# A linear-attention and feed-forward kernel: w3 laid out for 32x32 block turns on VectorE, seven products for one more chunk, another opening and another order of work

## The chip, the core and the metric

The kernel runs on one core of one Trainium2 chip. The metric is the device time of one execution in microseconds (us), lower is better. The engines are named as in the profile: PE (TensorE, matrix products; PEld are its weight loads), DVE (VectorE), ACT (ScalarE), POOL (GpSimd) and SP (SyncE, which here only issues DMAs). Each engine works through its own list of instructions in order and waits on semaphores for the others.

## The reference

Two blocks follow each other. The first is a recurrent linear attention over 4 batches, 8 heads, 768 steps and a head size of 48:

```python
for t in range(S):
    cur = np.einsum('bhd,bhe->bhde', u[None] * kt, vt)
    y[:, :, t] = np.einsum('bhd,bhde->bhe', rt, state + cur)
    state = w[None, :, :, None] * state + np.einsum('bhd,bhe->bhde', kt, vt)
```

Its output, reordered to x of 3072 tokens by 384, goes through a multiplicative feed-forward block. `w1` and `w2` are 384 x 1024, `w3` is 1024 x 1024, `w_out` is 1024 x 384:

```python
a = x @ w1
b = x @ w2
h = a * b @ w3
return (h @ w_out)
```

The weights arrive as 64-bit floats, so their transfers carry twice the bytes of 32-bit ones.

## The kernel before, in words

**Units and chunks.** The sequence is cut into 6 chunks of 128 steps. A chunk of one batch is a unit, so there are 24 units; the four units of a chunk give the 512 tokens of one feed-forward step. For each unit `scale` multiplies k and r by powers of w (tile `pn_in`, which the opening computes), `adds` and `products` form the sums over time, `state` carries the state on, `with_state` and `with_pairs` give y, and `turn_y`/`put_y` turn it into `xT`. From unit 5 on, k and r are turned by blocks on VectorE (`turn_blocks`, L492), written to memory (`turn_out`, L496) and read back in another order (`turn_places`, L504).

**Weights.** Nothing in the kernel multiplies with 64-bit floats. 32 pieces are loaded by `fetch` (L229) into three raw buffers in turn, `raws[i % 3]`: pieces 0 to 7 are strips of w1 and w2 (768 KB each), 8 to 15 are 128-row blocks of w_out (384 KB), 16 to 31 are half blocks of 128 rows of w3 (512 KB). Five steps rebuild 32-bit floats from the two words of each number: `magnitude` and `low` on ScalarE, `sign`, `high` and `total` on VectorE. A buffer is free for piece i + 3 when `low` has read it.

**Folding.** Since nothing stands between w3 and w_out, their product w34 is computed once: for each block j of 128 rows, `fold_turn` turns w3's block with eight 128x128 transposes on TensorE (L398), `fold_put` copies them out of PSUM (L403), `fold` multiplies by w_out (L408, eight products of 384 columns), `fold_take` copies the result to w34. The tiles `w3n` and `w3T` share four buffers of 4 KB per partition.

**Products.** For chunks 0 and 1 the products of x with w1 and w2 are plain ones (`product_ab`, L740: three products of 512 columns for each of 8 blocks of features and each weight). For chunks 2 to 5 seven half-size products take the place of eight (`product_half`, L885 and L889, 256 columns each, with `gather_half`), over two of the three blocks of 128 inputs; they need sums of quarters of the weights (`sums_of_w`) and of x (`sums_of_x`). The product of h with w34 is always done in seven parts (`product`, L798, `gather`).

**Order.** A string of 1406 words, `ORDER`, is the whole program of PE, ACT, DVE and SP for this case. A word is a step and its indices: `W.9` issues piece 9, `M`, `N`, `H`, `L`, `Q` convert it, `G.j.h`, `K.j.h`, `F.j`, `X.j` fold block j, `a.c.j.part`/`b.c.j.part` are plain products, `pa`/`pb` and `ga`/`gb` half-size ones, `P`, `E`, `D` the products with w34, their sums and stores, `k`, `T`, `R`, `U`, `A`, `S`, `V`, `Y`, `yt`, `x`, `y`, `z` and others the steps of a unit, `Z.n.i` n products that only keep TensorE busy. Steps on different engines wait for each other through the tiles they share; each engine keeps the order of the string. The order was written by a planner outside the kernel.

**Opening.** Before the string, VectorE builds powers of w by doubling in the tile `both`; two copies double its width (L297, L298), TensorE turns eight 128x128 blocks (L303), and ScalarE copies the two halves g into `pn_in` (L304). A branch then picks this program or a general one for other values of w; only the first is run here.

Of the kernel before, what the change touches and what calls it, by code (L numbers as in the profile page):

```python
# [8 lines left out]
F32 = mybir.dt.float32  # L9
# [14 lines left out]
k.0 uw Z.1.0 R.0 vs.0 T.0 k.1 kr.2 U.0 t.0 v.2 r.0 i.0 T.1 j.0 ku.0 A.0 R.1 N.0 v.1 Au.0 t.1 r.1 S.0 m.0 kr.3 ku.1  # L24
mo.0 k.2 Z.4.0 A.1 M.0 Au.1 fe.0 R.2 W.1 m.1 vs.2 T.2 mo.1 U.2 W.2 t.2 H.0 V.0 r.2 Y.0 v.3 A.2 i.2 j.2 ku.2 U.1 yt.0
kr.4 i.1 j.1 S.2 L.0 Au.2 k.3 yx.0 vs.1 Z.1.0 R.3 m.2 T.3 M.1 mo.2 S.1 fe.2 fe.1 t.3 V.2 N.1 V.1 r.3 H.1 Y.2 A.3 W.3
Q.0 ku.3 yt.2 N.2 kr.5 vs.3 Z.2.0 Au.3 Y.1 m.3 yx.2 Z.2.0 U.3 mo.3 M.2 yt.1 v.5 i.3 k.4 S.3 yx.1 L.1 a.0.0.0 fe.3 H.2
Q.1 M.3 V.3 W.4 T.4 N.3 Y.3 R.4 H.3 kr.6 t.4 yt.3 b.0.1.0 r.4 j.3 ku.4 k.5 A.4 v.6 cz.1 L.3 Au.4 x.5 b.0.0.0 yx.3 L.2
Q.3 a.0.1.1 M.4 N.4 W.5 Q.2 vs.5 W.6 H.4 c.0.0.0 c.0.1.1 Z.3.0 b.0.2.2 m.4 v.4 L.4 mo.4 W.7 vs.6 Q.4 d.5 a.0.2.2
u.0.0.0 y.5 N.5 M.5 H.5 U.5 c.0.2.2 a.0.1.0 u.0.2.2 L.5 ub N.6 M.6 Q.5 b.0.1.1 vs.4 W.8 H.6 b.0.4.2 c.0.1.0 u.0.1.0  # L30
L.6 u.0.1.1 Q.6 W.9 M.7 N.7 a.0.4.2 H.7 z.5 e.5 L.7 f.5 Q.7 M.8 a.0.7.2 c.0.4.2 N.8 H.8 M.9 N.9 W.10 L.8 H.9 W.11 Q.8
L.9 b.0.6.2 Q.9 c.0.7.2 W.12 h.5 kr.7 l.5 d.6 e.6 f.6 a.0.0.1 M.10 N.10 H.10 b.0.7.2 N.11 M.11 kr.8 u.0.4.2 L.10 H.11
c.0.0.1 L.11 Q.10 N.12 M.12 Q.11 a.0.5.2 W.13 H.12 L.12 W.14 k.7 Q.12 W.15 b.0.0.1 d.7 c.0.5.2 e.7 kr.10 f.7 A.5
u.0.0.1 b.0.3.2 i.5 M.13 N.13 H.13 N.14 L.13 m.5 M.14 W.16 H.14 a.0.6.2 M.15 Q.13 L.14 N.15 W.17 H.15 Q.14 L.15 Q.15
W.18 c.0.6.2 j.5 b.0.5.2 u.0.6.2 M.16 N.16 H.16 u.0.7.2 M.17 a.0.3.2 N.17 L.16 H.17 W.19 Q.16 L.17 N.18 M.18 W.20 Q.17
G.0.0 c.0.3.2 H.18 G.0.1 K.0.0 U.4 u.0.3.2 L.18 k.6 K.0.1 W.21 F.0 N.19 M.19 kr.9 Q.18 H.19 N.20 M.20 i.4 L.19 H.20
W.22 Q.19 L.20 Q.20 M.21 W.23 N.21 G.1.0 X.0 H.21 G.1.1 K.1.0 U.6 j.4 K.1.1 G.2.0 x.6 L.21 F.1 K.2.0 W.24 Q.21 M.22
y.6 N.22 H.22 k.8 L.22 M.23 W.25 N.23 H.23 Q.22 L.23 N.24 W.26 G.2.1 Q.23 M.24 S.4 z.6 x.7 K.2.1 G.3.0 X.1 G.3.1 fe.4
H.24 K.3.0 F.2 M.25 N.25 u.0.5.2 L.24 H.25 K.3.1 Q.24 L.25 y.7 Q.25 M.26 W.28 N.26 H.26 W.27 d.8 l.6 e.8 kr.11 G.4.1
G.4.0 L.26 x.8 A.6 K.4.0 V.4 i.6 X.2 F.3 Y.4 cz.0 v.7 M.28 m.6 K.4.1 j.6 z.7 M.27 N.28 H.28 Q.26 L.28 Q.28 N.27 H.27  # L40
S.5 X.3 G.6.0 vs.7 fe.5 y.8 G.5.0 K.6.0 W.29 P.0.0.0 L.27 Q.27 W.30 V.5 W.31 l.7 yt.4 Y.5 G.5.1 g.6 yt.5 v.8 F.4 z.8
N.29 M.29 f.8 yx.4 H.29 yx.5 N.30 L.29 d.9 K.5.0 Q.29 K.5.1 N.31 g.7 S.6 e.9 G.6.1 fe.6 V.6 K.6.1 U.7 Y.6 v.9 M.30 A.7
k.9 F.6 M.31 X.4 m.7 kr.12 l.8 i.7 j.7 vs.8 x.9 vs.9 H.30 y.9 H.31 L.30 Q.30 L.31 U.8 X.6 Q.31 S.7 A.8 fe.7 k.10 V.7
yt.6 z.9 m.8 G.7.0 yx.6 i.8 G.7.1 K.7.0 F.5 j.8 K.7.1 g.8 x.10 v.10 s.0.1.0 y.10 s.0.1.1 Y.7 s.0.1.2 l.9 f.9 d.10 yt.7
X.5 e.10 kr.13 ps f.10 yx.7 g.9 s.0.1.3 z.10 d.11 b.1.0.2 e.11 vs.10 f.11 d.12 e.12 a.1.0.2 b.1.1.2 c.1.0.2 u.1.0.2
a.1.5.2 a.1.1.2 c.1.5.2 b.1.2.2 c.1.1.2 u.1.1.2 a.1.2.2 a.1.4.2 c.1.2.2 u.1.2.2 S.8 c.1.4.2 U.9 fe.8 l.10 A.9 k.11
b.1.4.2 i.9 kr.14 j.9 m.9 x.11 U.10 A.10 u.1.4.2 y.11 V.8 k.12 F.7 v.11 i.10 kr.15 j.10 m.10 Y.8 z.11 x.12 vs.11
a.1.3.2 B.0 X.7 E.0.0.0 s.0.0.0 y.12 B.1 a.1.6.2 s.0.0.1 c.1.3.2 B.3 B.2 s.0.0.2 P.0.0.2 c.1.6.2 wb.0 wb.1 P.0.1.4
s.0.0.3 wa.0 P.0.0.3 wa.1 wb.3 P.0.1.2 wa.3 E.0.0.2 U.11 E.0.0.3 P.0.0.4 k.13 x.13 P.0.1.0 E.0.0.4 y.13 b.1.6.2
E.0.1.0 E.0.1.2 b.1.5.2 u.1.6.2 P.0.1.1 u.1.5.2 s.1.0.0 P.0.0.5 s.1.0.1 s.1.0.3 a.1.7.2 s.1.0.2 E.0.1.1 E.0.0.6  # L50
E.0.0.5 D.0.0.0 P.0.0.1 wa.2 c.1.7.2 P.0.0.6 E.0.0.1 b.1.3.2 E.0.0.7 D.0.0.1 P.0.1.6 u.1.3.2 P.0.1.3 P.1.0.0 E.0.1.3
E.0.1.4 yt.8 E.1.0.0 P.0.1.5 g.10 b.1.7.2 E.0.1.6 E.0.1.7 f.12 yx.8 D.0.1.1 d.13 e.13 kr.16 P.1.1.0 u.1.7.2 s.1.1.0
P.1.0.4 s.1.1.1 E.1.1.0 s.1.1.3 P.1.0.2 s.1.1.2 wb.2 P.1.0.6 E.1.0.2 E.0.1.5 D.0.1.0 P.1.0.3 P.1.0.5 E.1.0.3 E.1.0.4
P.1.1.1 E.1.0.6 E.1.0.5 D.1.0.0 P.1.1.4 E.1.1.1 P.1.0.1 P.1.1.2 E.1.0.1 E.1.0.7 D.1.0.1 S.9 E.1.1.2 P.1.1.3 fe.9 l.11
z.12 V.9 E.1.1.3 Y.9 A.11 P.1.1.5 i.11 j.11 yt.9 m.11 v.12 P.1.1.6 yx.9 E.1.1.6 g.11 E.1.1.4 E.1.1.5 S.11 D.1.1.0
E.1.1.7 S.10 D.1.1.1 fe.11 V.11 fe.10 l.12 f.13 V.10 v.14 Y.11 U.12 v.13 vs.12 Y.10 yt.11 k.14 z.13 pa.2.0.0 yx.11
x.14 A.12 ga.2.0.0 yt.10 i.12 pa.2.0.1 yx.10 m.12 g.12 j.12 xs.2.0 S.12 y.14 xs.2.1 U.13 fe.12 xs.2.2 ga.2.0.5 V.12
xs.2.3 g.13 pa.2.0.5 d.14 v.15 e.14 kr.17 pa.2.1.4 Y.12 f.14 pa.2.0.4 ga.2.0.1 d.15 l.13 e.15 pa.2.0.6 ga.2.0.3 vs.13
A.13 z.14 f.15 yt.12 ga.2.0.2 i.13 pb.2.0.0 vs.15 m.13 yx.12 pa.2.0.7 j.13 g.14 k.15 pa.2.0.3 ga.2.0.4 kr.18 x.15
vs.14 S.13 U.14 ga.2.0.7 fe.13 y.15 d.16 V.13 gb.2.0.0 k.16 pa.2.0.2 l.14 v.16 Y.13 e.16 kr.19 f.16 pb.2.0.5 ga.2.0.6  # L60
d.17 pa.2.1.0 e.17 gb.2.0.1 pb.2.0.6 x.16 z.15 pb.2.0.1 gb.2.0.2 vs.16 pb.2.0.3 gb.2.0.5 y.16 A.14 gb.2.0.7 yt.13 m.14
ga.2.1.0 pb.2.0.4 g.15 i.14 pa.2.1.5 j.14 pa.2.1.1 gb.2.0.3 ga.2.1.1 f.17 yx.13 d.18 l.15 pb.2.0.7 e.18 pb.2.1.0
ga.2.1.5 gb.2.0.4 z.16 pa.2.1.6 gb.2.0.8 U.15 ga.2.1.2 pb.2.0.2 k.17 x.17 kr.20 pa.2.1.3 gb.2.0.6 y.17 ga.2.1.3
s.2.0.0 pa.2.1.7 s.2.0.2 pa.2.1.2 ga.2.1.4 ga.2.1.7 gb.2.1.0 s.2.0.1 s.2.0.3 pb.2.1.4 ga.2.1.6 S.14 pb.2.1.1 fe.14
l.16 z.17 V.14 gb.2.1.5 A.15 Y.14 P.2.1.0 m.15 i.15 v.17 yt.14 E.2.1.0 j.15 pb.2.1.5 yx.14 g.16 S.15 U.16 fe.15 V.15
k.18 A.16 v.18 gb.2.1.1 P.2.0.0 Y.15 kr.21 l.17 gb.2.1.3 m.16 vs.17 pb.2.1.7 x.18 E.2.0.0 yt.15 pa.3.0.0 yx.15 i.16
y.18 g.17 pb.2.1.6 j.16 f.18 S.16 xs.3.0 U.17 xs.3.1 gb.2.1.2 A.17 fe.16 xs.3.2 vs.18 V.16 i.17 pb.2.1.3 v.19 j.17
z.18 m.17 gb.2.1.4 pb.2.1.2 gb.2.1.7 gb.2.1.8 ga.3.0.0 gb.2.1.6 pa.3.0.4 vs.19 s.2.1.0 pa.3.0.5 s.2.1.2 pa.3.0.1
ga.3.0.1 s.2.1.1 ga.3.0.3 l.18 s.2.1.3 pa.3.0.6 xs.3.3 ga.3.0.5 pa.3.0.2 k.19 ga.3.0.2 x.19 pb.3.0.0 Y.16 ga.3.0.6
y.19 d.19 S.17 e.19 kr.22 U.18 fe.17 f.19 A.18 i.18 V.17 pa.3.0.7 v.20 m.18 pa.3.0.3 ga.3.0.4 z.19 j.18 Y.17 P.2.1.1  # L70
ga.3.0.7 k.20 gb.3.0.0 d.20 P.2.0.3 e.20 vs.20 x.20 kr.23 P.2.0.2 E.2.1.1 P.2.0.5 y.20 E.2.0.2 E.2.0.3 l.19 pb.3.0.5
# [34 lines left out]
def kernel(  # L106
# [60 lines left out]

# [885 lines left out]
```

## Time and profile before

| | us |
|---|---|
| median of 3 runs | 507.02 |
| lowest and highest run | 500.76, 507.63 |
| profiled execution, time | 501.81 |
| profiled execution, span | 500.1 |
| PE busy | 483.8 |
| DVE busy | 319.5 |
| ACT busy | 202.7 |
| first product of chunk 1 starts at | 139.65 |
| last PE instruction ends near | 494.8 |

The profile shows one execution. A matrix product of 32-bit floats appears as two records, and records of neighbours overlap, so costs of products are read from the start-to-start distance of a row of them, not from the mean duration. Busy shares are means over stages that have different limits; a stretch of the span tells more. In a table of stretches "x" counts instructions, PEclk is the clock that was granted to TensorE, and DMA share is the mean over the 16 DMA engines. Packets that cross a border of a short stretch can lift the share above 1.

### The profile page before, as it was taken

What the parts mean: (1) busy time and instruction counts of PE and PEld (TensorE: products, weight loads), DVE (VectorE), ACT (ScalarE), POOL (GpSimd) and SP (SyncE); (2) the same over time, 40 slices, a digit from 0 to 9 for tenths busy, and PEclk for the clock granted to TensorE, in tenths of its full rate; (3) what the DMA queues carried; (4) which work ended last, traced back from release to release, by engine and by line L of the source; (5) the groups of instructions that cost most, each with busy time, mean ns of one, the idle gap of its engine ahead of it and who ended that gap; (6) DMA issues with size and microseconds to landing.
All of it is one profiled execution on the core that took longest, in us unless ns stands there. A gap on an engine that the chain in (4) does not pass through costs nothing.

```text
span 500.1 us, 11978 instructions
## 1 busy us (share of the span) xinstructions
PE 483.8 (97%) x5066; PEld 384.4 (77%) x5066; DVE 319.5 (64%) x648; ACT 202.7 (41%) x470; POOL 4.4 (1%) x17
## 2 busy tenths in 40 slices
PE   6899999989999999999999999999999999999995
PEld 5786545657644586898888889989998889888895
DVE  5799999985951874539967894539462564524352
ACT  3887646768632100206852633062422232322300
POOL 3000000000000000000000000000000000000000
PEclk9999999999999999999999999999999999999999
DMA  8969787896620600216734435002300020000002
GB/s 193 241 167 287 209 224 227 250 262 172 159 64 1 174 33 20 59 49 177 167 108 108 113 99 139 32 33 70 90 33 31 1 81 17 27 25 0 2 1 69
DMA packets 97279, 52.72 MB, mean 105 GB/s; under 512 B 78144, under 2 KB 88640, under 8 KB 97216
## 3 DMA queue, kind: packets, MB, share of 16 engines
q1 hardware_dynamic: 96592, 51.85, 37.6%
q8 instruction: 42, 0.69, 0.6%
q14 instruction: 21, 0.17, 0.1%
q10 hardware_dynamic: 624, 0.00, 0.1%
HBM read 39.65 MB, written 12.19 MB: 104 GB/s over the span
## 4 chain that ended last, share of the span: by engine, by line
PE 86%; DMA 5%; DVE 4%; ACT 2%; issue 1%; SPq 0%; ACTq 0%; DVEq 0%
PE ps_accB L885 8%; PE ps_b L740 7%; PE ps_a L740 7%; PE ps_w L408 5%; PE ps_a11b L798 3%; PE ps_s1t L798 3%; PE ps_s4b L798 3%; PE ps_s3t L798 3%; PE ps_a22t L798 3%; PE ps_s2t L798 3%; PE ps_a12b L798 3%; PE ps_Ab L885 3%; PE ps_accB L889 3%; PE ps_a L551 3%; PE ps_accC L885 3%; PE ps_Aa L885 3%
## 5 line engine op out<-in xcount | busy, mean ns | idle before, releaser
L740 PE MATMUL ps_b<-xT,w 128*128 128x512 f32 (+1 forms) x108 | 44.4, 550 | 0.9 <-ACT a L746 0.7
L740 PE MATMUL ps_a<-xT,w 128*128 128x512 f32 (+1 forms) x108 | 43.7, 547 | 0.0
L408 PE MATMUL ps_w<-wo,w3T 128*128 128x384 f32 x128 | 43.0, 489 | 0.0
L885 PE MATMUL ps_accB<-x,w 128*128 128x256 f32 x128 | 36.5, 387 | 0.0
L740 PEld LDWEIGHTS ps_a<-xT,w 128*128 128x128 f32 x108 | 20.3, 190 | 20.5 <-issue 18.4
L408 PEld LDWEIGHTS ps_w<-wo,w3T 128*128 128x128 f32 x128 | 23.7, 190 | 15.1
L452 ACT ACTIVATE ynat<-vnat,dg 128x48 f32<-128x48 f32 x144 | 34.4, 325 | 0.8 <-PE ps_x L710 0.7
L740 PEld LDWEIGHTS ps_b<-xT,w 128*128 128x128 f32 x108 | 19.9, 190 | 18.7 <-issue 15.8
L508 ACT COPY kT<-tt 128x1024 f32<-128x1024 f32 x19 | 19.9, 1047 | 23.3 <-PE ps_y L671 21.0
L382 ACT ACTIVATE t<-raw 128x512 uint32<-128x512 uint32 (+2 forms) x32 | 22.6, 710 | 14.6 <-DVE wo L378 6.7
L885 PEld LDWEIGHTS ps_accB<-x,w 128*128 128x128 f32 x128 | 23.2, 190 | 5.0 <-ACT u2a L902 1.1
L422 DVE TENSOR_TENSOR krs<-krin,pn_in 128x768 f32<-128x768 f32 x24 | 22.9, 953 | 5.9 <-PE ps_a L544 3.3
L749 DVE TENSOR_TENSOR abt<-ps_b,a 128x512 f32<-128x512 f32 (+1 forms) x18 | 11.2, 628 | 20.5 <-ACT a L746 14.0
L746 ACT COPY a<-ps_a 128x512 f32<-128x512 f32 (+1 forms) x18 | 9.5, 535 | 33.4 <-PE ps_a L740 33.3
L716 ACT COPY xT<-ps_x 128x384 f32<-128x384 f32 x24 | 11.4, 478 | 28.8 <-PE ps_x L710 28.6
L678 ACT COPY vodd<-vnat 64x192 f32<-64x192 f32 x48 | 16.8, 350 | 13.8 <-DMA vnat<-in_v_dram 12.8
L551 PE MATMUL ps_a<-kT 64*64 64x64 f32 x768 | 16.8, 222 | 3.0 <-ACT kT L508 1.7
L813 ACT COPY m<-ps_a11b 128x192 f32<-128x192 f32 x12 | 3.8, 320 | 38.7 <-PE ps_a11b L798 38.7
L492 DVE STREAM_TRANSPOSE tr<-krs 128x768 f32<-128x768 f32 x19 | 18.4, 970 | 1.1 <-DMA scratch<-tr 0.9
L602 DVE COPY_PREDICATED AT<-later,ps_a 128x512 f32<-128x512 int32 x24 | 17.5, 730 | 2.5 <-PE ps_a L572 1.4
L889 PE MATMUL ps_accB<-xT,w 128*128 128x256 f32 x64 | 19.0, 379 | 0.0
L889 PE MATMUL ps_accC<-xT,w 128*128 128x256 f32 x64 | 19.0, 379 | 0.0
(191 smaller groups left out, 1069.0 us busy)
## 6 DMA issues: line engine op xcount, KB each, us to landing
raw<-in_moe_w_dram SPq DMA_DIRECT2D x16, 512.0 KB, 4.9
scratch<-tr SPq DMA_DIRECT2D x19, 384.0 KB, 3.1
raw<-in_moe_w_dram SPq DMA_DIRECT2D x8, 768.0 KB, 5.8
tt<-scratch SPq DMA_DIRECT2D x38, 128.0 KB, 3.1
krin<-in_k_dram SPq DMA_DIRECT2D x24, 192.0 KB, 3.8
krin<-in_r_dram SPq DMA_DIRECT2D x24, 192.0 KB, 4.3
vnat<-in_v_dram SPq DMA_DIRECT2D x24, 192.0 KB, 3.8
raw<-in_moe_w_out_dram SPq DMA_DIRECT2D x8, 384.0 KB, 3.6
```

Source lines behind the costliest of these rows:

```text
L382: nc.scalar.activation(out=part["t", i], in_=words(i)[0], func=COPY, scale=2.0 ** -29)
L408: nc.tensor.matmul(ps, lhsT=w3T[j][:, kc, :], rhs=wo[kc], start=(kc == 0), stop=(kc == KF - 1))
L422: nc.vector.tensor_mul(krs[n % NS][:, which, :, :D], kr[:, which], pn[:, which, :, :D])
L452: nc.scalar.activation(out=ynat[n][:, h, :], in_=vnat[n % NV][:, h, :], func=COPY, scale=dg[n][:, h:h + 1])
L492: nc.vector.transpose(out=blocks[n].rearrange("x m e t -> x e m t"), in_=krs[n % NS][:, :, :, :D])
L508: nc.scalar.copy(out=turned(n).rearrange("x g p (z t) -> x (g p) z t", t=Q), in_=tts.rearrange("x z e t -> x e z t"))
L551: nc.tensor.matmul(upper(n)[rows(a ^ i), i, p, :], lhsT=kT[n][rows(i), p, rows(a)], rhs=rT[n][rows(i), p, rows(a)], start=True, stop=True)
L602: nc.vector.copy_predicated(AT[n], later.bitcast(I32)[:, None, None, :].to_broadcast([C, 2, NP, T]), upper(n))
L740: nc.tensor.matmul(ps, lhsT=(w1 if x == "a" else w2)[:, z, q, js], rhs=xT[c][:, q, ts], start=(q == 0), stop=(q == KM - 1))
L798: nc.tensor.matmul(ps, lhsT=operand(c, j // 2, a)[:, j % 2, m * C:(m + 1) * C], rhs=w34[:, KH * (x == 1) + j, :DH] if x < 2 else made[b][: ...
L885: nc.tensor.matmul(ps, lhsT=quarter(w, g, i, x), rhs=(b11, b21, b22, t4, b12, t2, t3)[x], start=x in (0, 4) and i == 0, stop=True, skip_gr ...
L889: nc.tensor.matmul(ps, lhsT=wide_of[w][:, g + half * HZ, 2, i * P:(i + 1) * P], rhs=xT[c][:, 2, side * TH:(side + 1) * TH], start=False, s ...
```

## The change

Three parts and a new order.

**w3 and w_out are loaded in another layout.** A piece of w3 is now two transfers. Each brings 32 rows of w3, and each of the four groups of 32 partitions takes another quarter of the columns. In that layout a turn of 32x32 blocks within each group gives what a 128x128 transpose gave, with the inner index of the product permuted; the rows of w_out are loaded with the same permutation. `fold_turn` becomes one block turn on VectorE for each half, and `fold_put` (word `K`) goes.

```diff
+            if i < NAB + KF:
+                queue.dma_start(out=landed[i] if i < NAB else landed[i][:, 0], in_=pieces[i])
+            else:
+                j, z = divmod(i - NAB - KF, NW3)
+                for f in range(2):
+                    queue.dma_start(out=landed[i][:, 0, f * DF // NBLOCK:(f + 1) * DF // NBLOCK],
+                                    in_=moe_w3[j * P:(j + 1) * P].rearrange("(f r) (q x) -> f q r x", r=Q, q=NBLOCK)[2 * z + f])
...
-    pieces = [src for src, _ in strips] + [moe_w_out[j * P:(j + 1) * P, None, :] for j in range(KF)] \
+    pieces = [src for src, _ in strips] + [moe_w_out.rearrange("(q c x) n -> c q x n", q=P // Q, x=Q)[j] for j in range(KF)] \
...
-            pst["w3", j, h] = ps = psT.tile([P, KF // 2, P], F32, tag="t", name=f"ps_w3T{j}_{h}")
-            for q in range(KF // 2):
-                kc = h * (KF // 2) + q
-                nc.tensor.transpose(ps[:, q, :], w3n[j][:, kc * P:(kc + 1) * P], ident)
+            if j not in w3T:
+                w3T[j] = wide_pool.tile([P, KF, P], F32, tag="w3", bufs=4 if fast else 3, name=f"w3T{j}")
+            by = w3n[j].rearrange("x (f c r) -> x f c r", f=NBLOCK, r=Q)[:, 2 * h:2 * h + 2]
+            nc.vector.transpose(out=w3T[j].rearrange("x c (f r) -> x f c r", r=Q)[:, 2 * h:2 * h + 2], in_=by)
```

Here `P` is 128, `Q` is 32, `NBLOCK` is 4, `KF` is 8 and `NW3` is 2.

**Chunk 1's products with w1 and w2 are half-size ones too** (`pa.1`, `pb.1`, `ga.1`, `gb.1` in place of `a.1`, `b.1`, `c.1`, `u.1`). The sums of w1, w2 and x that they need take the four shared buffers of w3 when the folding is done (`kept`, `more_kept`), since the memory of the other pools is full then.

```diff
-                made["w", w] = [room().tile([P, HZ, STRIP], F32, name=f"w{w}{i}") for i in (1, 2, 4)]
+                made["w", w] = [kept(3 * (w == "b") + i) for i in range(3)]
...
-                made["x", c] = [room().tile([P, TH], F32, tag=f"x{i}", name=f"x{i}_{c}") for i in (2, 3, 4)]
+                made["x", c] = [more_kept(i * TH, TH) for i in range(3)]
```

**The opening is rewritten at its end.** `both` isn't doubled any more; 16 products with the identity write each of the 8 blocks to both halves of the partitions, and the second copy into `pn_in` is VectorE's. A constant tile shares its memory with a raw buffer. The first unit's `scale` is split into k and r.

```diff
-        nc.vector.tensor_copy(out=both[:, 0, :, T:], in_=both[:, 0, :, :T])
-        nc.scalar.copy(out=both[:, 1, :, T:], in_=both[:, 1, :, :T])
-
...
-                nc.tensor.transpose(ps[:, p, :], both[:, g, p, :], ident)
-            nc.scalar.copy(out=pn_in[:, g].rearrange("t h d -> t (h d)"), in_=ps.rearrange("x p t -> x (p t)"))
+                for a in range(2):
+                    nc.tensor.matmul(ps[rows(a), p, :], lhsT=both[:, g, p, :T], rhs=ident, start=True, stop=True)
+            put = nc.vector.tensor_copy if g else nc.scalar.copy
+            put(out=pn_in[:, g].rearrange("t h d -> t (h d)"), in_=ps.rearrange("x p t -> x (p t)"))
```

**The order** is a new string of 1426 words. Ahead of chunk 1's products it now has all of the folding, with `F.7` before `F.5`, and the first of the products with w34. Fillers fall from 13 products to 3. Part of it, where the folding ends:

```
... Q.30 G.7.0 s.0.1.0 L.31 Q.31 l.7 s.0.1.1 vs.7 z.8 G.7.1 S.6 X.6 wa.0 U.7 g.7 A.7 fe.6 wa.2 V.6 i.7 F.7 ...
... V.7 F.5 v.10 m.8 f.8 z.9 x.10 g.8 d.9 wb.3 Y.7 vs.10 y.10 i.8 kr.12 j.8 yt.7 B.0 X.5 P.0.1.0 yx.7 l.9
xs.1.0 xs.1.1 P.0.1.1 xs.1.2 E.0.1.0 z.10 xs.1.3 E.0.0.0 s.0.0.0 pb.1.0.4 ...
```

## The prediction, made before the result was known

> **What bounds the kernel now.** I read the page's busy shares first, then a table of stretches of the span, the chain that ended last, the waits, and last the DMA issues.
>
> ```profile
> span 500.1 us, 11978 instructions
> PE 483.8 (97%) x5066; PEld 384.4 (77%) x5066; DVE 319.5 (64%) x648; ACT 202.7 (41%) x470; POOL 4.4 (1%) x17
> DVE  5799999985951874539967894539462564524352
> DMA  8969787896620600216734435002300020000002
> ```
>
> TensorE is the bound by its share, but the third and fourth line say that VectorE and the DMA engines are nearly as full over the first quarter. The stretches show it in microseconds (stretch, length, busy time of PE, PEld, DVE, ACT, POOL, clock, DMA share, GB/s):
>
> ```profile
> 10.50:75.00 64.50, 61.83 (x888) 41.68 (x888) 56.29 (x101) 45.47 (x96) 0.00 (x0) 1.00 0.81 225
> 75.00:111.50 36.50, 33.94 (x275) 21.21 (x276) 32.99 (x62) 24.02 (x43) 0.00 (x0) 1.00 0.83 245
> 111.50:139.65 28.15, 27.96 (x416) 19.31 (x414) 21.50 (x45) 21.25 (x55) 0.00 (x0) 1.00 0.57 159
> 139.65:172.00 32.35, 32.25 (x263) 16.44 (x264) 14.81 (x29) 7.16 (x19) 0.00 (x0) 1.00 0.33 73
> 44.00:46.00 2.00, 2.00 (x6) 0.90 (x5) 2.00 (x5) 1.42 (x3) 0.00 (x0) 1.00 1.03 367
> 76.00:78.00 2.00, 2.00 (x6) 0.88 (x5) 1.90 (x5) 0.00 (x0) 0.00 (x0) 1.00 0.87 283
> 118.00:120.00 2.00, 2.00 (x8) 1.21 (x7) 1.91 (x4) 1.98 (x6) 0.00 (x0) 1.00 1.10 350
> ```
>
> 139.65 us is where TensorE begins the products of chunk 1; I call that moment X. Before X, VectorE is busy 110.8 of 129.15 us, from 75 to 111.5 us even 33.0 of 36.5. The DMA engines are 81 to 83% busy until 111.5 us. After X only TensorE is full. Over 69 to 106 us the chain runs through weight pieces, not through TensorE:
>
> ```profile
> 73.37 5.06 DMA raw<-in_moe_w_dram
> 80.61 4.98 DMA raw<-in_moe_w_dram
> 91.53 5.11 DMA scratch<-tr
> 97.97 6.35 DMA tt<-scratch
> ```
>
> SyncE's queue waits, before it may issue a piece, for the step `low` that empties the raw buffer (first line); the others are the pieces and their time to land:
>
> ```profile
> SPq L234 <- ACT t L382: 46.1, 23, 5.7
> raw<-in_moe_w_dram SPq DMA_DIRECT2D x16, 512.0 KB, 4.9
> raw<-in_moe_w_out_dram SPq DMA_DIRECT2D x8, 384.0 KB, 3.6
> ```
>
> So the pieces are now paced by the conversion that frees buffers. How fast are the 16 engines? The last three stretches above are mostly weights: 367/1.03, 283/0.87 and 350/1.10 GB/s are 318 to 356 at full share, 20 to 22 GB/s per engine. In the trace's packet records the median 2 KB packet takes 84 ns (24.4 GB/s), a 3 KB packet 121 ns, a 192 B packet 15 ns.
>
> [...] This trace has the operation itself in f32: 128x768 in 970 ns (L492), which I use. [...] Here the granted clock is 1.00 in every stretch of work[...].
>
> **The change, part by part.**
>
> *TensorE.* The 64 transposes of w3 (L398) go: eight cost 0.87 us back to back, four 0.44, so 7.0 us. Fillers (L921) fall from 13 products to 3: a pair of records is 0.216 us, so 2.2 us of filler. Chunk 1 as seven products: per weight and half of the features, 12 products of 512 columns at 0.859 us (2.58 us for three) become 22 of 256 columns at 0.431 (1.29 for three): 10.31 against 9.48, four times, 3.3 us less. Sum 12.5 us, if TensorE stays the bound.
>
> *VectorE and ScalarE.* 16 puts of w3T leave ScalarE (16 x 0.58 = 9.3 us). 16 block turns of 128x512 come onto VectorE: from 970 ns for 768 elements, 0.65 us each, 10.4 us (0.60 to 0.75 as ends). Seven weight sums (0.69 each), `B.0` and two halves of x now stand ahead of chunk 1's products: 4.8 + 1.0 + 0.8; 5.0 us of `d`, `e`, `f` and sums go behind. Adding durations in list order gives 121.7 us of VectorE before X in the old list and 134.0 in the new one; the trace's 111.8 us for what had run by X makes one list microsecond 0.932 (neighbours overlap). New VectorE work before X: 124.9 us.
>
> *Opening.* Two copies (0.30, 0.41) go, 16 half-width products replace 8 transposes (1.07 us for eight now; 0.9 to 1.7 for each g, by whether halves overlap), the second put goes to VectorE beside ScalarE's (0.59), and the first scaling is cut in two. I start the list at 9.7 us instead of 9.4, with some 1.7 us of VectorE work more done by 16 us: within 2 us either way.
>
> *DMA: the part that decides.* w3's 16 pieces become 32 transfers: source 4 blocks of columns, 32 rows, 256 words, so its outermost dimension is 4; the 8 pieces of w_out likewise (4, 32, 384). The destination has 128 partitions. [...] The bytes stay: w3 8.39 MB, w_out 3.15 MB, together 11.53 MB, so 2.88 MB on each. [...] at 24.4 GB/s 118, at 20 GB/s 144. I take 22.5: **128 us**. Spread over 16 they took 32. The four engines also carry their sixteenth of what SyncE issues among these pieces: three k and r pairs (128 packets per engine, 15.5 ns: 2.0 us each), one v (1.0), three scratch writes (1.4), one reading back (1.4): 12.6 us. The extra issues cost SyncE 16 x 0.35 us, beside waiting.
>
> **The sum.** The first w_out piece goes out when the seventh strip is converted, at 48.8 us before; the new list has about as much VectorE work ahead of it, so 49. Plus 2 for the first landing, 128, 12.6: the last piece lands at 192. Add 3 for a bubble: `z.6` makes SyncE wait for a scratch write, which lies behind pieces on the four engines, and `W.27` stands behind it; on `W.27` wait ScalarE's `M.26`/`M.27`, then VectorE's `H`, the turns and all of VectorE's list behind them. Then 3 for converting piece 31, and the new list's rest until chunk 1: 18.7 list us on VectorE (17.4), with `F.7` and `F.5` (5.16 each) and units 6 to 8 on TensorE crosswise: 20. X = 49 + 2 + 128 + 12.6 + 3 + 3 + 20 = **218** instead of 139.65.
>
> After X, the old list took 360.45 us. The new one has 3.3 us less of chunk 1, and `F.7` and two products (5.16 + 2.6) have moved ahead of X: 349.4. Later chunks have the same work, VectorE keeps slack there (53 list us against 76 of TensorE in chunk 1), and the last 5.1 us are stores. 218 + 349.4 = 567.4, against 500.1: **67 us more**. Counted from the profiled execution (501.81) that is 569; the median of the runs is 507.02, 1% higher, and I forecast on it: 574, rounded down to 573 because the puts that leave ScalarE shorten conversions a little. All TensorE savings ahead of X are worth nothing here: TensorE waits for pieces.
>
> **Rivals.**
>
> *The transfers spread over 16 engines after all, and VectorE becomes the bound ahead of X.* For it: VectorE's 33.0 of 36.5 us, and nothing in this trace shows a transfer on four engines. X = 9.7 + 124.9 + idle time. VectorE was idle 18 us before X, some 8 of it after 111.5 us, when it waited for a full TensorE; without those, 10 to 12. X = 146, total 495.4, so 4.7 less: 502 on the median, no change by the bound of 2%, which is about what a measurement of this kernel tells from none. With all 18 idle us: X = 152.6 and 509.
>
> *TensorE stays the bound everywhere.* All 12.5 us are gained: 487.6, 494 on the median, faster by over 2%. This is the end on the other side. It needs the 16-engine spread and VectorE idle under 3 us before X (X below 138.7); the 4.4 us that it idles from 10 to 25 us alone, on the first units' latency, speak against it.
>
> *VectorE's turns bring waits both ways:* TensorE's in-order list holds `U`, `A`, `S`, `V` behind an `F` that waits for a turn, and VectorE's `i`, `m`, `Y` wait for those. With 15 us of such idle time on top, X = 161: 510 or 517 on the median.
>
> **Chances.** Confined to four engines, 573: 0.84[...]. VectorE as bound, 502: 0.11. TensorE as bound, 494: 0.03. Mutual waits, 517: 0.02. Hence faster 0.03, same 0.11, slower 0.86. [...] 144 us, k, r and v transfers that queue behind pieces on the four engines[...] give 605. A range of 525 to 607 holds all but a twentieth of this case, 0.80 in all.
>
> **What would show it.** In the profile after: a DMA share near 0.25 to 0.35 from 50 to 190 us at some 80 to 100 GB/s; twice as many w3 issues with landings of 6 us and more where several are queued; ScalarE's `M` and VectorE's `N` waiting for raw in long steps; VectorE below 70% busy and TensorE below 60% there, with a clock under 1.00; chunk 1 beginning after 200 us, and from there a stretch of about 349 us. Right in any case: no L398 transposes, 16 block turns near 0.65 us, chunk 1's product time 3 us shorter. I am wrong if w3 lands at 250 GB/s or more: then X is near 146 and the total is within 2% of before. I am wrong in size if the four engines carry clearly over 24 GB/s each.

## The result, and the profile after

The changed kernel takes **567.72 us** (median of 4 runs, 563.78 to 569.26) against 505.21 us for the kernel before, run beside it (median of 4, 500.76 to 507.63). The ratio is **1.124, with a 95% interval of 1.113 to 1.134**: slower, as forecast, and 5 us short of the 573 us.

The page of the changed kernel, its span, busy shares and two of its lines of slices:

```profile
span 567.4 us, 12069 instructions
PE 495.1 (87%) x5086; PEld 401.5 (71%) x5086; DVE 335.3 (59%) x677; ACT 200.5 (35%) x462; POOL 4.4 (1%) x17
PEclk9989687779587799999999999999999999999999
DMA  8996223222434235205046615550203101000001
```

The DMA engines are 0.8 to 0.9 busy for the first three slices (43 us), much as before, and 0.6 in the fourth. Then their share drops to 0.2 to 0.4 and stays there through slice 13 (184 us), and over the same slices TensorE's granted clock is 0.5 to 0.9. Before, the share stood at 0.6 to 0.9 for eleven slices (138 us), and then the weights were in.

The stretches of the changed kernel (stretch, length, busy time of PE, PEld, DVE, ACT, POOL, clock, DMA share, GB/s):

```profile
50.00:85.00 35.00, 24.11 (x73) 9.39 (x71) 19.49 (x40) 12.68 (x22) 0.00 (x0) 0.80 0.30 107
85.00:192.00 107.00, 61.10 (x337) 32.90 (x341) 48.98 (x89) 26.47 (x48) 0.00 (x0) 0.79 0.33 107
192.00:220.00 28.00, 28.00 (x367) 19.61 (x360) 24.09 (x47) 15.10 (x45) 0.00 (x0) 0.90 0.45 115
```

For 142 us nothing is full: TensorE is busy 57% of the second stretch, VectorE 46%, the DMA engines 33%, and memory delivers 107 GB/s where it gave 245 before. That fits transfers that run on a few of the engines. The chain that ended last and two lines of the waits say what is waited for (waits: engine, tile and line, what ended the wait; total us, times, longest):

```profile
PE 69%; DMA 21%; DVE 3%; ACT 3%; issue 2%; SPq 1%; DVEq 0%; ACTq 0%
ACT w3n L380 <- DMA raw<-in_moe_w_dram: 59.0, 10, 15.7
DVE t L385 <- DMA raw<-in_moe_w_dram: 50.5, 14, 11.3
```

A fifth of the chain is now weights in flight. X, the start of chunk 1's products, in the timeline of TensorE, and the block turns among the groups by form (count, busy us, mean ns):

```profile
218.74 1.03 PE L914 MATMUL ps_Fb<-xT,sumw 128*128 128x256 f32 x4
...
L414 DVE STREAM_TRANSPOSE w3T<-w3n 128x512 f32<-128x512 f32 x16 | 11.1, 702 | 0.2
```

X went from 139.65 to 218.74 us. From X to the end it is 348.7 us, against 360.45 before. So 79.1 us were lost ahead of X and 11.8 us won behind it.

### The profile page after: what moved, and what is told of

The parts are those of the page before. It is cut to its first block, busy times and chain, and to the rows that moved or that the text cites. A ratio compares the mean times of both kernels' runs of the same rounds, so it can differ in the third digit from the quotient of the medians.

```text
span 567.4 us, 12069 instructions
## 1 busy us (share of the span) xinstructions
PE 495.1 (87%) x5086; PEld 401.5 (71%) x5086; DVE 335.3 (59%) x677; ACT 200.5 (35%) x462; POOL 4.4 (1%) x17
## 4 chain that ended last, share of the span: by engine, by line
PE 69%; DMA 21%; DVE 3%; ACT 3%; issue 2%; SPq 1%; DVEq 0%; ACTq 0%
DMA raw<-in_moe_w_dram 15%; PE ps_accB L914 10%; DMA raw<-in_moe_w_out_dram 5%; PE ps_Ab L914 3%; PE ps_w L419 3%; PE ps_accC L914 3%; PE ps_Aa L914 3%; PE ps_accB L918 3%; PE ps_accC L918 3%; PE ps_s3t L809 3%; PE ps_a22t L809 3%; PE ps_s4b L809 3%; PE ps_a12b L809 3%; PE ps_s1t L809 3%; PE ps_s2t L809 3%; PE ps_a11b L809 3%
## 5 line engine op out<-in xcount | busy, mean ns | idle before, releaser
L385 DVE TENSOR_SCALAR t<-raw 128x512 uint32<-128x512 uint32 (+2 forms) x32 | 14.0, 442 | 65.2 <-DMA raw<-in_moe_w_dram 50.5
L751 PE MATMUL ps_b<-xT,w 128*128 128x512 f32 (+1 forms) x60 | 30.6, 663 | 19.2 <-ACT a L757 10.9
L914 PE MATMUL ps_accB<-sumw,w 128*128 128x256 f32 x160 | 45.3, 385 | 0.0
L914 PEld LDWEIGHTS ps_accB<-sumw,w 128*128 128x128 f32 x160 | 29.2, 190 | 4.7 <-ACT u3a L931 0.6
L751 PE MATMUL ps_a<-xT,w 128*128 128x512 f32 (+1 forms) x60 | 25.5, 565 | 7.3 <-DVE abt L760 7.3
L433 DVE TENSOR_TENSOR krs<-krin,pn_in 128x768 f32<-128x768 f32 (+1 forms) x25 | 22.8, 920 | 2.6 <-PE ps_a L555 2.4
L914 PE MATMUL ps_accC<-xT,sumw 128*128 128x256 f32 x80 | 24.1, 383 | 0.0
L914 PE MATMUL ps_Ab<-xT,w 128*128 128x256 f32 x80 | 22.6, 385 | 0.0
L914 PE MATMUL ps_Aa<-xT,w 128*128 128x256 f32 x80 | 22.4, 382 | 0.0
L914 PE MATMUL ps_accB<-sumw,sumw 128*128 128x256 f32 x80 | 21.3, 388 | 0.0
```

The source lines that it names most:

```text
L385: nc.vector.tensor_scalar(part["t", i], words(i)[1], 0x80000000, None, ALU.bitwise_and)
L433: nc.vector.tensor_mul(krs[n % NS][:, which, :, :D], kr[:, which], pn[:, which, :, :D])
L751: nc.tensor.matmul(ps, lhsT=(w1 if x == "a" else w2)[:, z, q, js], rhs=xT[c][:, q, ts], start=(q == 0), stop=(q == KM - 1))
L914: nc.tensor.matmul(ps, lhsT=quarter(w, g, i, x), rhs=(b11, b21, b22, t4, b12, t2, t3)[x], start=x in (0, 4) and i == 0, stop=True, skip_gr ...
```

## The experiments

**1. Is it the four engines?** The theory, which was the author's assumption in the prediction: the transfers of w3 and w_out run on four DMA engines because their outermost dimension is 4. The rival: something else in the change is slow, and the low DMA share only follows. Four kernels tell these apart.

Both weights spread again: the same bytes to the same places, but one transfer for each block of 32 partitions, with an outermost dimension of 32. The first kernel does it for both weights, the second for w_out alone, and leaves w3 as changed.

```diff
-  queue.dma_start(out=landed[i][:, 0], in_=pieces[i])                      # w_out: 4 x 32 x 384
+  for q in range(NBLOCK):
+      queue.dma_start(out=landed[i][q * Q:(q + 1) * Q, 0], in_=pieces[i][q])
...
-  for f in range(2):                                                       # w3: 4 x 32 x 256
-      queue.dma_start(out=landed[i][:, 0, f * DF // NBLOCK:(f + 1) * DF // NBLOCK], in_=...[2 * z + f])
+  for q in range(NBLOCK):
+      queue.dma_start(out=landed[i][q * Q:(q + 1) * Q, 0].rearrange("r (f x) -> r f x", f=2),
+                      in_=...rearrange("(f r) (q x) -> q r f x", r=Q, q=NBLOCK)[q][:, 2 * z:2 * z + 2])
```

> The changed kernel with one edit: each piece of w3 and of w_out is brought by four transfers, one for each group of 32 partitions, so that the outermost dimension is 32 on both sides. Bytes, rows, 2 KB and 3 KB packets, block turns, order and everything else stay. Theory (the four-engine confinement is the whole loss): the DMA share of the first quarter is back above 0.7, VectorE is the bound ahead of chunk 1, which begins near 146 us (140 to 153), and the span is near 495 us (490 to 502), 2% or less from the kernel before. Rival 1 (the new order and the waits between VectorE and TensorE cost it): chunk 1 begins after 190 us and the span stays above 540. Rival 2 (small packets or the rows' pitch in memory are slow in themselves): the packets keep their number and size, so the span stays above 540 as well.

> The changed kernel with w_out alone spread by four transfers of 32 partitions; w3 keeps its outermost dimension of 4. Theory: the eight pieces of w_out land at the pace of the conversions again, done by about 75 us instead of 92, and w3's 95 us on four engines start that much earlier: chunk 1 near 203 us (198 to 208), span near 552 us (546 to 558). Rival (order and waits): within 3 us of the changed kernel's 567.4.

Both spread: 510.91 us median, ratio 1.011 (1.002 to 1.020), span 508.2, X at 159.95. Only w_out spread: 557.35 us in one run, span 555.6, X at 207.60. So spreading takes back 59.2 of the 67.3 us of span, 11.8 of them with w_out and the rest with w3. The expectation of the first was missed all the same: X is 14 us later than 146, and the span is above the 490 to 502 us. The second part of this section goes after that.

The other two go the opposite way. One is to halve the engines again, by four transfers of 64 rows for each w3 piece, whose outermost dimension is 2. The other takes the kernel *before* and changes nothing but the order in which a w3 piece's rows are read.

```diff
# the changed kernel, w3 on two engines
+  for f in range(2):
+      for h in range(2):
+          queue.dma_start(out=landed[i][2 * h * Q:2 * (h + 1) * Q, 0, f * DF // NBLOCK:(f + 1) * DF // NBLOCK],
+                          in_=...rearrange("(f r) (q x) -> f q r x", r=Q, q=NBLOCK)[2 * z + f, 2 * h:2 * h + 2])
# the kernel before, w3 on four engines
-  queue.dma_start(out=landed[i], in_=pieces[i])
+  queue.dma_start(out=landed[i][:, 0],
+                  in_=moe_w3[j * P:(j + 1) * P, z * PIECE:(z + 1) * PIECE].rearrange("(r q) x -> q r x", q=P // Q))
```

> The changed kernel with w3 in four transfers per piece, each with an outermost dimension of 2 (two groups of 32 partitions); w_out stays at 4. Theory: w3 now goes over two engines, 4.19 MB on each instead of 2.10, at the 93 ns per 2 KB packet of the changed kernel 190 us instead of 95: span near 660 us (640 to 680), DMA share near 0.2 while w3 loads. Rivals (order, packets, pitch, or that the number of transfers does not matter): within 10 us of 567.4.

> The kernel before, with its own order, its transposes on TensorE and its 4 KB packets; only the rows of each 128-row block of w3 are loaded in another order, so that the source's outermost dimension is 4. Each half block stays one transfer. The rows of w3 are exchanged within a block, so the output is another one; all work is the same. Theory (confinement alone does it): 16 pieces at 32 packets of 160 to 203 ns are 82 to 104 us on four engines, the last piece lands near 181 us instead of 121, chunk 1 begins near 194 us and the span is near 555 us (540 to 570). Rival (the block turns, the new order or the seven products of chunk 1 make the loss): within 10 us of 500.

With two engines: 652.32 us, span 650.6 (one run). The kernel before with w3 on four engines: 561.63 us, span 559.9 (one run). Both lie inside what was expected, as does the one with w_out alone spread. The stretch of the two-engine kernel in which w3 loads, and X of the other (the row that stood at 139.65):

```profile
100.00:270.00 170.00, 67.10 (x324) 35.27 (x322) 45.59 (x82) 23.30 (x41) 0.00 (x0) 0.66 0.19 63
```
```profile
198.65 2.84 PE L744 MATMUL ps_b<-xT,w 128*128 128x512 f32 x6 [0.19 <-ACT xT L720]
```

The share drops from 0.33 to 0.19 and the rate from 107 to 63 GB/s with an outermost dimension of 2 in place of 4. In the kernel before, whose VectorE turns nothing of w3 and whose list of work is untouched, an outermost dimension of 4 for w3 alone cost 59.8 us of span. The rival has no place for either, so this dimension is shown as the cause.

That it means four engines shows in the packet records. In the changed kernel exactly four packets of 2 KB are under way in 64% of the time from 100 to 190 us, and more than five in under 1%; for 3 KB packets, those of w_out, from 52 to 92 us it is 68% and under 1%. In the kernel before up to 16 of w3's 4 KB packets are under way at a time from 75 to 120 us, and more in 3% of it. The updates of the semaphores that report transfers as landed fall as well. In the kernel before there are 3648, 16 for each of its 228 transfers. In the changed kernel there are 3464: 16 for each of 204 transfers and 5 for each of the 40 of w3 and w_out, one update 0.4 us after the issue has ended and four as the data lands. A w3 transfer on two engines leaves 3, and the counts of all four kernels (3472 in the kernel before on four engines, 3496 on two) come out exactly. That each engine leaves one of them, and the issue another where there are fewer than 16, is the author's reading.

With four and two engines taken as given, their speed can be read from ScalarE's first step on w3's pieces, 15 pieces or 7.86 MB apart: 88.3 to 190.0 us in the changed kernel (19.3 GB/s per engine), 85.5 to 179.5 in the kernel before on four (20.9), 96.9 to 274.1 on two (22.2). These are w3's bytes alone; other transfers ran in between.

**2. What is left when the engines are spread?** The spread variant is at 1.011, where the prediction's rival for 16 engines had it at 0.99. Three suspects: SyncE issues 96 transfers for w3 and w_out where the kernel before issued 24; VectorE has more to do; the order of work is new. The kernels: the change without its w3 part; the sign of w3's pieces moved from VectorE to ScalarE (in this one w3 loses its signs, the work is otherwise the same); half of w3's transfers issued by GpSimd; and the kernel before with nothing but four transfers in place of one.

```diff
# without the w3 part (each K directly after its G, two PSUM slots for chunk 1 taken after the last K)
-  moe_w_out.rearrange("(q c x) n -> c q x n", q=P // Q, x=Q)[j]      and w3 by blocks of columns
+  moe_w_out[j * P:(j + 1) * P, None, :]                              and queue.dma_start(out=landed[i], in_=pieces[i])
-  fold_turn on VectorE          ... G.0.0 ...
+  fold_turn on TensorE, fold_put on ScalarE   ... G.0.0 K.0.0 ...
# sign on ScalarE, in the order of work
-  N.16 ... N.31
+  n.16 ... n.31
# GpSimd
-  queue.dma_start(out=landed[i][q * Q:(q + 1) * Q, 0]...
+  (queue if q < 2 else nc.gpsimd).dma_start(out=landed[i][q * Q:(q + 1) * Q, 0]...
# the kernel before, more transfers
-  queue.dma_start(out=landed[i], in_=pieces[i])
+  for q in range(4 if i >= NAB else 1):
+      rows = slice(q * P // 4, (q + 1) * P // 4) if i >= NAB else slice(0, P)
+      queue.dma_start(out=landed[i][rows], in_=pieces[i][rows])
```

(The first expectation counts the transfers wrongly: the spread variant has 96, and the variant without the w3 part has 24, for 16 pieces of w3 and 8 of w_out.)

> The change without its w3 part: w3 and w_out are loaded in their own order again (32 w3 pieces and 8 w_out pieces, each one transfer over all 128 rows), TensorE turns w3 (64 transposes, 7.0 us) and ScalarE copies the result out (16 copies, some 12 us); the opening, the sums, the seven products of chunk 1 and the new list stay (the step that takes two PSUM slots for chunk 1 stands after the last copy). Beside it stands the spread variant, with chunk 1's products from 159.95 us and a span of 508.2. If the spread variant is late because its 128 small transfers are issued one after the other on SyncE (40 us of issuing), the 40 transfers here bring X to 145-150 and the span to 493-499. If it is late because VectorE's list before X is too long, the 11 us of block turns that leave VectorE give X of 147-151, the same span within 3 us: this run doesn't separate the two, the others of this set do. If the new list itself is what is late, whatever w3 does, X stays at 157-162 and the span at 505-510.

> The spread variant (w3 and w_out over all 16 DMA engines, X at 159.95, span 508.2) with one step of each w3 piece, the sign, moved from VectorE to ScalarE: 16 instructions, about 0.425 us each on VectorE, about 0.7 on ScalarE. If VectorE's work is what is late before X: X falls by the 6.8 us that leave it, to 152-155, span 501-504. If the late thing is the w3 pieces' arrival, behind their issuing on SyncE: X stays within 2 us of 160, or rises by up to 5 since ScalarE's chain of a piece is longer; span 506-513.

> The spread variant with two of the four transfers of each w3 piece issued by GpSimd, which is idle, and two by SyncE: 32 of 64 issues (0.425 us each, 13.6 us) leave SyncE's queue. If the issuing on SyncE is what delays the pieces: X falls from 159.95 by 5-12 us, to 148-155, span 496-503. If VectorE's list is what is late: X stays within 2 us, span 506-510. A cost on GpSimd's side (its issue is not in any trace so far) would show as later landings and a longer span, 510-515.

> The kernel before with nothing changed but the number of transfers: each of the 8 w_out and 16 w3 pieces is four transfers of 32 rows instead of one of 128 rows, from the same places to the same places (96 issues in place of 24, so 72 more, at about 0.42 us each 30 us more of issuing on SyncE). If issuing on SyncE delays the pieces in the spread variant, it does here: X goes from 139.65 to 145-154, the span from 500.1 to 506-514. If it doesn't, X stays within 2 us and the span within 2 us of the kernel before.

| kernel | median us | ratio to before (95%) | X, us |
|---|---|---|---|
| both weights spread | 510.91 | 1.011 (1.002 to 1.020) | 159.95 |
| change without its w3 part | 514.27 | 1.017 (1.011 to 1.022) | 169.25 |
| spread, sign on ScalarE | 507.90 | 1.007 (1.004 to 1.010) | 163.23 |
| spread, half the w3 issues on GpSimd | 505.82 | 1.003 (1.001 to 1.005) | 155.37 |
| before, four transfers per piece | 510.15 | 1.011 (1.007 to 1.015) | 145.75 |

The last two bear on **the issues**. Their rows in the kernel before with four transfers, and in the GpSimd variant (shortest, median, longest ns, first and last start). The last row of each fence is w_out's in the kernel that it is set against, the kernel before and the spread variant:

```profile
L236 SPq DMA_DIRECT2D raw<-in_moe_w_dram x72: 310/419/1528, 5.3 to 123.6; - x72
L236 SPq DMA_DIRECT2D raw<-in_moe_w_out_dram x32: 311/419/1157, 50.6 to 72.4; - x32
...
L234 SPq DMA_DIRECT2D raw<-in_moe_w_out_dram x8: 328/334/746, 48.8 to 66.1; - x8
```
```profile
L246 SPq DMA_DIRECT2D raw<-in_moe_w_dram x32: 311/390/887, 68.9 to 124.7; - x32
L246 POOL DMA_DIRECT2D raw<-in_moe_w_dram x32: 533/533/766, 69.1 to 125.1; - x32
L242 SPq DMA_DIRECT2D raw<-in_moe_w_out_dram x32: 310/419/644, 50.6 to 72.3; - x32
...
L242 SPq DMA_DIRECT2D raw<-in_moe_w_out_dram x32: 310/419/425, 53.2 to 75.4; - x32
```

A piece is complete only when its fourth transfer has been issued, 1.3 us after the first, and the other loads in SyncE's queue stand behind all four. Cutting the transfers alone makes the kernel before 1.1% slower, as expected. In its profiled execution X is 6.1 us later, but 1.8 of them were lost before the first cut transfer was issued (50.6 us against 48.8). Whether the issuing costs the rest or the larger number of transfers, this pair doesn't tell.

With half of w3's issues on GpSimd, which is free (although one takes 0.53 us there), the spread variant stands at 1.003 instead of 1.011; the intervals overlap. Its X of 155.37 us lies between the two ranges expected, 148 to 155 and within 2 us of 159.95. And of the 4.6 us that X is earlier, 2.6 are there at the first w_out issue (50.6 us against 53.2), up to which both kernels do the same. How much an idle engine's queue takes back is thus not shown; 2.0 us is what is left for it here.

The other two were inconclusive. The sign on ScalarE leaves 507.90 us, better than 510.91 but inside the interval of the other, and the profiled execution was a long one of its ten (512.78 us), so its X says nothing. The change without its w3 part reaches X later than any expectation had it, and has this line among its waits up to 160 us:

```profile
ACT w3T L412 <- PE ps_w3T L407: 22.1, 12, 4.3
```

ScalarE waits 22.1 us for TensorE's turns, which I put down to each copy standing right behind its turn, and its profiled execution was 1% above its own median. It shows only that the new order with the copies placed so, w3 on TensorE, is 1.7% slower than the kernel before.

**3. The order, or who turns w3?** Now the order of work before goes in front: the old list up to 139.65 us, stand-in products included, and then the new list without what is done by then. Once with w3 turned on TensorE from whole pieces (so the seven products of chunk 1 and the shorter opening are all that is left of the change), once with VectorE turning and GpSimd issuing, and once as the first but with the transfers of the second.

```diff
# in the change without its w3 part, and in the GpSimd variant
-  ORDER = the new list
+  ORDER = the list before up to g.8 ... z.10 d.11, then wa.0 wa.2 F.7 wa.1 wa.3 wb.0 ... of the new list
# VectorE turning: its turn stands where ScalarE's copy stood
-  G.0.0 G.0.1 K.0.0 ... K.0.1
+  G.0.0 ... G.0.1
# third kernel: TensorE turning, more transfers
-  queue.dma_start(out=landed[i], in_=pieces[i])
+  for q in range(4 if i >= NAB else 1):
+      by = nc.gpsimd if i >= NAB + KF and q > 1 else queue
+      by.dma_start(out=landed[i][rows], in_=pieces[i][rows])      # rows as above
```

> One part of the change alone, the seven products of chunk 1, with the shorter opening: w3 and w_out in their own order, one transfer for each piece, TensorE turns w3 and ScalarE copies it out, as in the kernel before; the order of work is the list before up to the point where chunk 1's first product stood (139.65 us), its stand-in products included, and from there the new list, without what has been done by then. Between the two stand the fold of the last w3 block (5.4 us of TensorE), three small products of chunk 0 and VectorE's 14 sums, so chunk 1's first product is due at 146-150 us. If the early part of the new list is what loses time in the spread variant and in the one with w3 turned on TensorE (X at 159.95 and 169.25), this kernel loses none of it: it gains what TensorE saves, 3.3 us for chunk 1 and up to 3 in the opening, for a span of 493-498 and a ratio of 0.985-0.995. If the sums of chunk 1 on VectorE, ready too late, are what loses time, TensorE waits for them after 140 us and the span is 500-506.

> The variant whose w3 loads are spread and issued half by SyncE and half by GpSimd (X at 155.37, span 503.6), VectorE turning w3, with the order of work before in front: the list before up to 139.65 us, each VectorE turn at the place of ScalarE's copy, with the stand-in products, then the new list without what has been done by then. Only the order of the work before chunk 1 differs from that variant. If the early part of the new list is what costs the rest: VectorE works at 56-57 of the 65 us from 10 to 75 us again and chunk 1's first product comes at 144-151 us, span 493-500. If VectorE's longer work before X (11 us of turns) is what costs it: the first product stays at 153-158 and the span at 501-506.

> The variant with the seven products of chunk 1 alone (TensorE turns w3; chunk 1's first product at 154.44 us, 501.49 us median, ratio 0.994) with its transfers cut as in the variant with the order before and VectorE's turns (160.73 us, 510.95 us median, ratio 1.015): four transfers of 32 rows for each w3 and w_out piece, two of each w3 piece issued by GpSimd. Those two then differ in who turns w3, and in 4 KB against twice 2 KB of each row. If the number of transfers is what costs the 9.5 us between them, this run has a ratio of 1.007-1.015 (507-511 us) and its first product of chunk 1 at 158-161. If VectorE's 11 us of turns are what costs them, it stays at 0.992-0.999 (500-503) and 154-156.

| old order in front | median us | ratio to before (95%) | X, us |
|---|---|---|---|
| TensorE turns, one transfer per piece | **501.49** | **0.994 (0.992 to 0.997)** | 154.44 |
| TensorE turns, four transfers, half of w3's on GpSimd | 504.43 | 0.999 (0.996 to 1.001) | 155.81 |
| VectorE turns, four transfers, half of w3's on GpSimd | 510.95 | 1.015 (1.012 to 1.019) | 160.73 |

The first is the fastest kernel of this study, 0.6% under the kernel before. Its page begins:

```profile
span 502.1 us, 12199 instructions
PE 483.9 (96%) x5170; PEld 403.9 (80%) x5170; DVE 325.4 (65%) x660; ACT 208.3 (41%) x478; POOL 4.4 (1%) x17
```

(This execution took 503.79 us, 2.3 more than the median of its 17 runs.) It met the ratio expected, but X came 4 to 8 us later than expected, and the span of its median run, 499.7 us, is above the 493 to 498. (X can't be compared with 139.65 here: the last fold and VectorE's sums for the seven products now stand ahead of it.)

The third row differs from the second in who turns w3 and in the cut of the rows. The stretch from 75 us to X, and the row of X, for VectorE turning and then for TensorE turning:

```profile
75.00:160.70 85.70, 72.20 (x670) 43.18 (x668) 76.14 (x145) 44.43 (x100) 17.33 (x32) 0.94 0.76 182
...
160.73 1.13 PE L916 MATMUL ps_Fb<-xT,sumw 128*128 128x256 f32 x4 [1.67 <-DVE xT L889]
```
```profile
75.00:155.80 80.80, 74.08 (x730) 47.24 (x729) 65.54 (x126) 51.59 (x115) 15.74 (x32) 1.00 0.75 189
...
155.81 1.13 PE L915 MATMUL ps_Fb<-xT,sumw 128*128 128x256 f32 x4 [0.67 <-DVE xT L888]
```

VectorE, 65.5 us busy when TensorE turns w3, is 76.1 us busy when it turns w3 itself: 10.6 more, about its 16 turns. TensorE has only 1.9 us less to do, at a lower clock, and ScalarE 7.2. In both rows TensorE's last wait before X is for VectorE. X comes 4.9 us later, of which 1.5 are there at the first w_out issue (54.0 us against 52.5), and the time is 1.6% longer: **the turn was moved onto the engine that X waits for**. That the turns make the difference is argued from these lines. The cut of the rows may have a part in it, which no run separates; VectorE waits 4.0 us for w3's transfers in the first stretch and 2.9 us in the second.

My expectation for the VectorE row had X at 144 to 151 us if the order was the cause and at 153 to 158 if VectorE's turns were. It lies beyond both, and the order as the cause is refuted: the old order with VectorE's turns (1.015) is slower than the new one (1.003). The new order was worth 1.2% to a kernel that turns on VectorE. Set against each other at their best, 1.003 and 0.994, each with the order that suits it, the w3 part costs 0.9% even without the four engines, about half of it by its transfers, if they cost there what they cost with TensorE turning (0.999 against 0.994).

## Why the prediction was right

**The four engines and the 128 us** held. That an outermost dimension of 4 would mean four engines was the author's assumption, and the trace of before couldn't show it. The runs bear it out, with 2 (63 GB/s), 4 (107 GB/s) and 32 (59.2 us of span taken back), and in the unchanged kernel too (59.8 us more). Which engines they are, and that w3 and w_out share the same four, no trace here tells. With the mean durations of all packets of these sizes in the changed kernel's trace, w3's 1024 packets of 2 KB per engine take 95 us (92.8 ns) and w_out's 256 of 3 KB 33.5 us (131 ns): 128.5. The first w_out piece was issued at 49.7 us (forecast 49), and w3's last transfer landed at 190.0 (forecast 192), where ScalarE began on it: 140 us in all, 142.6 forecast with the other loads on these engines.

**The 26 us from there to X** (bubble, last conversion, rest of the list) were 28.7. X came at 218.74 us, 218 forecast; the two small errors cancel. **The rest after X** was 348.7 us, 349.4 forecast, and the span 567.4, as summed.

**The 5 us that the forecast is too high** are in the last step, the scaling to the median. I added 1% because the profiled execution of before (501.81 us) lay that far under its median of 507.02. Beside the changed kernel the median of before was 505.21, and the profiled execution of the changed kernel (569.26 us) lies above its own median.

**The signs to look for**: DMA share 0.30 to 0.33 (0.25 to 0.35 forecast) at 107 GB/s (80 to 100 forecast, a little low); VectorE busy 48% from 50 to 190 us (below 70% forecast), TensorE 61% (below 60% forecast, just missed); clock 0.79 to 0.80. By the semaphore updates, w3's transfers landed 5.4 to 15.2 us after their issue began, 31 of the 32 after more than 6 us, as forecast for queued ones.

**The clock.** That it would fall below 1.00 was the author's assumption: in the kernel before it stays at 1.00 from 4.0 to 499.0 us, and no wait of TensorE between 10 us and the last product is longer than 1.73 us. In the changed kernel it goes to half (0.50) ten times before 197.7 us, for 3.4 to 13.7 us each, within waits of TensorE or behind them (the shortest 1.90 us). In the GpSimd variant no wait between 10 us and the last product is longer than 2.78 us, and the clock still went to half three times, for 3.4 us each, after waits of 2.78, 2.30 and 2.21 us. The first of them:

```profile
33.33 0.28 PE L586 MATMUL ps_a<-kT,tt 64*64 64x64 f32 x3 [2.78 <-issue]
34.30:37.70 3.40, 3.40 (x54) 2.74 (x53) 3.10 (x7) 3.40 (x9) 0.00 (x0) 0.50 0.81 181
```

A wait of 2.68 us in the kernel before with four transfers did not lower it, so no length of wait that decides can be read from these runs. The 0.90 of the changed kernel's last stretch above, in which TensorE is never idle, is half the clock (0.50) up to 197.7 us and 1.00 from there, after a wait of 3.9 us just before the stretch. The ends of the forecast's range, 525 and 607 us, are the author's estimates.

**The block turn.** A block turn of 128x512 took 0.702 us, not 0.65 (ends 0.60 to 0.75): 16 of them 0.8 us more.

**The first rival was wrong in its idle time.** VectorE's work ahead of X came out right: 125.25 us busy in the spread variant, 124.9 worked out. (The factor of 0.932 in that sum doesn't follow from the figures beside it: 111.8/121.7 is 0.92, which gives 123.1 us.) The stretch from 10 us to X, of the spread variant:

```profile
10.00:159.95 149.95, 129.26 (x1528) 82.18 (x1529) 125.25 (x232) 85.03 (x181) 0.00 (x0) 0.95 0.73 188
```

But VectorE idled 25 us in it, not the 10 to 12 that I left it, so that X was 159.95 and not 146. (The prediction took off 8 us of idle time after 111.5 us; its own line has 6.7.) Some 4 of the 14 us are there at the first w_out issue, 53.2 us where I had 49: TensorE's stops up to 75 us are 4 us longer than in the kernel before (below). The price of cutting transfers to spread them, which I had not put into this rival, was 4.3 us in the kernel before from the first cut transfer to X. The remaining 5 to 6 us are not assigned, and that these parts simply add up is not shown. For the spread variant the step "opening: within 2 us either way" is thus too narrow; in the changed kernel it held. From 10 to 75 us VectorE is busy 52.4 us in the spread variant and 55.8 with GpSimd, against 56.8 before.

**The rival on the other side**, 12.5 us of TensorE savings, needed VectorE to have room ahead of X. In part 3 it is busy 76.1 of 85.7 us once it turns w3, and X waits for it; of all that was to be saved, 0.6% is had, by leaving w3 where it was. (The rival's bound, X below 138.7 us, would leave VectorE 4.1 us of idle time after 9.7 + 124.9, not under 3.)

## What to carry to other kernels

Before rearranging a load, look at the outermost dimension that the rearrangement leaves: 4 in place of 128 made 11.5 MB of weights take 140 us instead of 72, from the first issue to the last landing, in a stretch whose DMA engines were already 80% busy. Spreading it by more and smaller transfers has a price too: four for one made the kernel before 1.1% slower. And work that leaves the engine with the highest share of the whole span only helps if the engine that takes it has room in the stretch where it lands: here VectorE, busy for 76.1 of 85.7 us with w3's turns, had little, and the time was 1.6% longer than with TensorE turning.

## What was unexpected

**Issuing itself took up to 7.6 us.** In the changed kernel SyncE's issues for w3, and one k and r load among them, seen in the timeline and in the rows of the tile (two engines last):

```profile
86.51 7.59 SPq L218 DMA_DIRECT2D krin<-in_r_dram  x1
...
L243 SPq DMA_DIRECT2D raw<-in_moe_w_dram x32: 531/532/7162, 77.2 to 183.0; - x32
```
```profile
L246 SPq DMA_DIRECT2D raw<-in_moe_w_dram x64: 506/2036/5072, 80.8 to 262.6; - x64
```

An issue on four engines takes 531 ns at the least, where one on sixteen took 346 ns in the kernel before (median) and 334 ns still does for w_out in the kernel before with only w3 on four engines. When pieces are queued, the issue goes on for up to 7.2 us, for the load of r, whose shape is unchanged, 7.6 us; with two engines the median is 2.0 us. Long issues are not confined to few engines: with all transfers on sixteen, in the change without its w3 part, the longest of a weight piece takes 3.9 us. What the queue waits for in that time the trace doesn't show.

**TensorE stops with nothing to wait for.** In the spread variant, within a run of equal small products:

```profile
27.55 0.22 PE L708 MATMUL ps_y<-vnat,AT 64*64 64x48 f32 x1
30.94 0.25 PE L708 MATMUL ps_y<-vodd,AT 64*64 64x48 f32 x1 [3.18 <-issue]
```

From 10 to 75 us such waits add up to 5.8 us there, and to 3.9, 6.7 and 6.7 us in the three other variants of part 2 that have the new order, but to 2.5 us in the changed kernel, which has it too. With the old order they are 1.8 to 3.7 us (kernel before, the same with four transfers and with w3 on four engines, and the three of part 3). So the order alone doesn't make them.

The traces point to a cause, **that TensorE waits for its own instructions**, but don't show it. Among the DMA packets are some of 16 KB of the kind "instruction" on queue 8, 42 in each trace, with some 250 of TensorE's records (products and weight loads) between one and the next. In the 13 traces there are 27 such stops over 0.6 us from 10 to 75 us, and every one ends 2.25 to 2.63 us after one of these packets has started. In the stop above the packet starts at 28.31 us, takes 1.0 us, and TensorE goes on at 30.94. Most of the 91 such packets in these stretches stop nothing. VectorE works on until 30.26 us here, and ScalarE waits for TensorE. No run was made to test this, and why such a packet goes with a stop at some places and not at others stays open; the DMA engines are 84 to 94% busy from 10 to 40 us.
